# Attention and two FFN layers on one core: one local-attention tile moves from TensorE blocks to VectorE, and the hand-written order list is laid out anew

## The chip, the cores and the metric

The kernel runs on one core of one Trainium2 chip. The metric is the device time of one execution in microseconds (us). PE is TensorE, DVE VectorE, ACT ScalarE, POOL GpSimd, and SP is SyncE, which issues most of the DMAs. Lower is better.

## The reference

The attention works on q, k and v of shape (4 batches, 8 heads, 576 positions, 64 channels). Its output is the sum of two parts, and two FFN layers follow:

```python
q_d, k_d, v_d = (z.reshape(B, H, 144, 4, D).mean(axis=3) for z in (q, k, v))
out_up = np.repeat(sm_attn(q_d, k_d, v_d), 4, axis=2)        # pooled attention
mask = np.abs(pos[:, None] - pos[None, :]) < 4               # local attention, 7 keys a query
out_local = softmax(np.where(mask, 0.125 * q @ k.T, -1e9)) @ v
x = (out_up + out_local)                                     # as (2304 tokens, 512)
x = np.maximum(x @ w_in, 0) ** 2 @ w_out                     # 2048 hidden channels
y = ((x @ w_a) * (x @ w_b)) @ w_out2                         # 1536 hidden channels
```

## The kernel before, in words

The 2304 tokens are nine attention tiles of 256 (i = 0 to 8). The first FFN takes them in pairs, `TILES = ((0, 2), (2, 2), (4, 2), (6, 2), (8, 1))`: four FFN tiles of 512 tokens and a last one of 256. For FFN tile t and each of 16 slices f of the hidden channels, `hidden` (token `H.t.f`, twelve matmuls of 128x512, L650) makes the hidden values, `highs` and `lows` (`J`, `L`) split them into two parts on ACT and DVE (L657 to L665), and `project` (`P.t.f`, twelve matmuls, L685) adds them into four PSUM banks, which `evict` (`E`) and `store` (`D`) move out. Then comes the second layer (L932 and around it), which the change touches only in which of its preparing steps (`F`, after `V.n` in numbered slots) stand where.

Local attention has two forms. `Block` works on PE: it loads queries, keys and values of two channel pairs cp (`bq`, `bv`), makes scores (`bs`, 16 matmuls a call, L530), a masked softmax on DVE, ACT and POOL (`bm`, `bx`, `be`, `bd`, `bn`; `be` is eight exponentials, L559), transposes (`bt`, 4 a call, L581, copied by `bc`), multiplies by the values (`bw`, 32 a call, L593), adds the pooled part (`bo`, `ba`) and splits into high and low (`bh`, `bl`). One tile has 4 calls of `bs`, 4 of `bt` and 2 of `bw`. `Local` works on DVE: for each of four heads it multiplies queries by a window of keys (`lm`, L418, 128x1792), reduces (`ls`, L426), and after a softmax (`lx`, `le`, `lz`) multiplies by a window of values (`lv`, L458); POOL adds the seven products up in three steps (`lw`, L468 to L470); PE transposes the result (`lt`, 4 matmuls, L476, two calls a tile), DVE adds the pooled part (`la`, L485), and it is split (`lh`, `ll`, L492, L498). It loads through `lk`, `lu` and `lb`. Tiles 0 to 4 are blocks and 5 to 8 local before the change (`BLOCKS = 5`).

Pooled attention runs per batch b: the four members of each group are added up in DRAM order by four DMAs, the first on SP (L264), the other three on POOL as accumulating DMAs that wait for one another (`pa.b.n.j`, L262; n = 0 is queries and keys together, n = 1 values). Batch 0 loads them apart and adds on DVE and POOL (`pg`, `pj`). Then `pq` scales, and `ps` (8 matmuls, L287), `px`, `pe`, `pd`, `pn`, `pt` (4, L338), `pc`, `pw` (8, L352), `po` follow. FFN tile t needs attention tiles 2t and 2t + 1, and the batches that lie in them.

The weights of the first FFN come as 64-bit words and are decoded by `wd` (the load, L215, into rings of a few buffers), `wc`, `wa` (L224), `wh`, `wl` (L235). `Z.k.n.kind` is n transposes of the identity (L872), which give nothing to the result.

What sets the order is the list `ORDER`. The program walks it from left to right and emits what each token names, with the letter at its end (A, V, G, S) choosing ACT, DVE, POOL or SP. Each engine runs its own instructions in that order and stops at one whose inputs or buffer aren't ready; SP does the same with its DMAs. `CTS` lets a pair of blocks take its channel tiles as 0, 1, 2, 3 and a pair of locals as 0, 2, 1, 3; FFN tile 2 (attention tiles 4 and 5) goes from the one to the other with the change.

Of the kernel before, what the change touches and what calls it, by code (L numbers as in the profile page):

```python
# [46 lines left out]
bs.1.0.0.5 wc.8.A wa.0 wh.0.G ps.0.0.1.6 wl.0.G ps.0.3.0.3 px.0.1.1 pe.0.1.1 bn.0.1.V px.0.2.1 ps.0.3.1.1 bv.0.0.S
px.0.0.0 pa.0.1.2 wd.1.S pe.0.2.1 wd.15.S bm.1.0.0 bx.1.0 pd.0.2 pd.0.1 wd.2.S pe.0.0.0 bt.0.0.1.2 px.0.3.1 bv.1.0.S
be.1.0 bc.0.0.1.A bs.1.0.1.7 px.0.0.1 bs.1.1.1.0 wc.1.V wa.1 pn.0.1.G bd.1.0 bt.0.1.1.4 pe.0.0.1 bn.1.0.G Z.0.4.5
pa.0.1.3 px.0.3.0 bm.1.0.1 pd.0.0 wc.15.V pn.0.0.V pn.0.2.A pe.0.3.1 Z.6.4.6 wh.1.V bm.1.1.1 bt.1.0.0.5 pt.0.2.0.6  # L50
bw.0.0.7 pe.0.3.0 wl.1.G bc.1.0.0.A wa.15 wh.15.G pt.0.0.1.5 pt.0.0.0.1 bt.1.1.0.3 pd.0.3 pt.0.1.0.2 bc.0.1.1.A bx.1.1
# [5 lines left out]
wh.17.G ba.1.1.V bh.1.2.A bh.0.2.A wa.5 bh.1.3.V bl.0.2.V bl.1.3.V bl.1.2.V H.0.0 wd.9.S bs.2.1.0.6 wh.5.V wl.5.V
H.0.1 J.0.0 bs.2.0.0.7 wc.3.V wa.3 wh.3.G wd.6.S bq.2.1.S wc.9.V wa.9 wl.3.V wd.10.S L.0.0 H.0.2 wa.4 wh.9.V P.0.0
wh.4.V wl.4.G wl.17.G J.0.1 wc.6.V L.0.1 H.0.3 wc.10.A wa.6 P.0.1 wl.9.G wh.6.A J.0.2 wd.7.S L.0.2 wl.6.G wc.7.A wa.10
wa.7 wh.7.V wl.7.G H.0.4 J.0.3 wd.11.S wh.10.G wl.10.V wc.11.V wa.11 wh.11.V wl.11.V pl.1 bm.2.1.0 wd.14.S L.0.3 P.0.2  # L60
wc.14.V H.0.5 wa.14 wd.13.S wd.12.S wc.12.A P.0.3 wh.14.G wl.14.V wc.13.A wa.13 J.0.4 wa.12 L.0.4 H.0.6 bm.2.0.0
wh.13.G wl.13.V wh.12.V wl.12.V bx.2.0 bs.2.1.1.7 wd.16.S wc.16.A wa.16 wh.16.G pa.1.1.0 pa.1.0.0 J.0.5 L.0.5 wd.19.S
H.0.7 P.0.4 P.0.5 wc.19.A be.2.0 wa.19 wd.24.S wd.22.S wh.19.V J.0.6 wc.24.V wa.24 L.0.6 pa.1.0.1 H.0.8 bd.2.0 P.0.6
bn.2.0.V bm.2.1.1 bs.2.0.1.6 J.0.8 wd.21.S wc.21.V pa.1.1.1 wa.21 L.0.8 bm.2.0.1 wh.21.A bx.2.1 wh.24.V wl.16.G
wl.19.G H.0.10 wd.18.S wd.20.S wd.25.S J.0.7 L.0.7 H.0.9 wl.21.G wc.20.A bt.2.1.0.7 pa.1.0.2 P.0.7 wc.18.A wa.18
wh.18.V wl.18.V P.0.8 wa.20 bc.2.1.0.A wc.22.V wh.20.G wc.25.A wl.20.G J.0.9 L.0.9 wa.22 H.0.11 wh.22.A P.0.9 wa.25
wh.25.V J.0.10 ps.1.0.0.7 wl.22.V wd.29.S L.0.10 wc.29.V wa.29 pa.1.0.3 pq.1.V ps.1.0.1.0 J.0.11 be.2.1 px.1.0.0
wl.25.G bt.2.0.0.6 bd.2.1 wd.26.S wl.24.V L.0.11 P.0.10 wd.23.S px.1.0.1 wc.26.A ps.1.1.0.1 wc.23.A P.0.11 wa.26
pe.1.0.1 bc.2.0.0.A pe.1.0.0 bn.2.1.G wa.23 wh.26.V bt.2.1.1.6 pa.1.1.2 wh.23.V wl.23.V bv.2.0.S bc.2.1.1.V bw.2.0.0
bo.2.0.A wd.27.S bq.3.0.S wc.27.A ps.1.1.1.7 bt.2.0.1.6 H.0.12 wa.27 bc.2.0.1.A px.1.1.0 bv.2.1.S wh.29.V bw.2.1.6  # L70
pe.1.1.0 pd.1.0 px.1.1.1 H.0.13 pn.1.0.A J.0.12 wd.28.S wh.27.V bo.2.1.V L.0.12 pe.1.1.1 wc.28.A wl.26.G ps.1.2.0.7
pt.1.0.0.6 pt.1.0.1.0 J.0.13 pc.1.0.0.A wl.27.V P.0.12 ps.1.2.1.6 pc.1.0.1.V wa.28 wd.31.S wh.28.A wc.31.V wa.31
pd.1.1 H.0.14 pn.1.1.V px.1.2.1 pe.1.2.1 pa.1.1.3 wl.29.G wl.28.V wd.30.S px.1.2.0 pe.1.2.0 wh.31.V wl.31.V L.0.13
pw.1.0.7 pt.1.1.1.1 wc.30.A pc.1.1.1.A po.1.0.A wa.30 pt.1.1.0.1 ps.1.3.0.7 ps.1.3.1.6 wh.30.A wl.30.G pd.1.2
pc.1.1.0.A pn.1.2.G P.0.13 px.1.3.1 px.1.3.0 J.0.14 bv.3.0.S bq.3.1.S pw.1.1.1 L.0.14 bs.3.1.0.0 pe.1.3.0 pe.1.3.1
po.1.1.A pd.1.3 ba.2.0.G bs.3.1.1.1 pt.1.2.1.7 pc.1.2.1.A bh.2.0.V bs.3.0.0.6 pt.1.2.0.7 bh.2.1.A pn.1.3.A pc.1.2.0.A
bm.3.1.1 bm.3.1.0 bm.3.0.0 bx.3.0 be.3.0 H.0.15 pt.1.3.1.6 bs.3.0.1.7 bm.3.0.1 pw.1.2.0 J.0.15 bx.3.1 bl.2.1.V
pc.1.3.1.A P.0.14 bd.3.0 pt.1.3.0.7 bn.3.0.V bt.3.0.0.6 be.3.1 bc.3.0.0.A pc.1.3.0.V L.0.15 bt.3.1.0.7 bc.3.1.0.V
pw.1.3.1 bw.3.0.6 P.0.15 po.1.3.V bd.3.1 pl.2 bl.2.0.V bn.3.1.V po.1.2.A pa.2.0.0 bq.4.0.S bv.3.1.S bt.3.1.1.0
pa.2.0.1 bo.3.0.A bt.3.0.1.1 pa.2.0.2 ba.2.1.V E.0.1.V pa.2.0.3 E.0.0.A pa.2.1.0 lu.20 bh.2.3.A bl.2.3.V ps.2.0.0.6  # L80
bc.3.0.1.A bc.3.1.1.V ba.3.0.V bs.4.1.0.7 bw.3.1.3 bh.2.2.A D.0.0 lk.22 Z.5.4.1 bl.2.2.V bh.3.0.V bs.4.0.0.2 bo.3.1.A
ba.3.1.V bh.3.1.A bh.3.2.A bm.4.1.0 ps.2.1.0.3 bl.3.0.G bh.3.3.A bl.3.1.G bl.3.3.V E.0.2.V bl.3.2.G pq.2.A bm.4.0.0
H.1.0 ps.2.1.1.7 H.1.1 J.1.0 px.2.1.0 pa.2.1.1 bx.4.0 L.1.0 H.1.2 pe.2.1.0 lm.5.2 J.1.1 be.4.0 px.2.1.1 E.0.3.V L.1.1
lk.20 bd.4.0 P.1.0 P.1.1 pe.2.1.1 H.1.3 ls.5.2 lm.5.0 J.1.2 L.1.2 bq.4.1.S ls.5.0 ps.2.0.1.7 D.0.1 H.1.4 bn.4.0.G
pa.2.1.2 P.1.2 px.2.0.1 lk.21 J.1.3 px.2.0.0 lm.5.1 L.1.3 ls.5.1 pa.2.1.3 H.1.5 pe.2.0.1 lk.23 J.1.4 L.1.4 pe.2.0.0
bt.4.0.0.7 H.1.6 P.1.3 pd.2.0 J.1.5 lm.5.3 P.1.4 ls.5.3 pd.2.1 bc.4.0.0.A lx.5 pn.2.0.G pt.2.0.0.6 bv.4.1.S bs.4.0.1.7
# [1233 lines left out]
```

## Time and profile before

| | us |
|---|---|
| median of 3 runs | 916.7 (916.36 to 917.46) |
| the profiled execution | 917.33 |
| its span, first to last instruction | 915.3 |
| PE busy | 884.0 |
| DVE, ACT, POOL busy | 567.0, 444.0, 305.5 |

The profiled execution lasted 2.0 us longer than its span. The first FFN begins at 53.3 us of the span (first matmul of L650), its FFN tiles 1, 2, 3 and 4 at 169.38, 278.72, 371.45 and 460.98, and the second layer at 512.95. The mean granted clock of PE, as a share of 2.4 GHz, is 0.81 over the first 53.3 us and 1.00 in every later stretch.

### The profile page before, as it was taken

The numbers are of one execution on the slowest core, as the hardware profiler recorded it, in microseconds if no ns is written. First come the engines' busy times: TensorE is split into PE (matmuls) and PEld (weight loads), VectorE is DVE, ScalarE is ACT, GpSimd is POOL, SyncE is SP. The second block draws the span as 40 slices with busy tenths as digits, with TensorE's granted clock in tenths as the row PEclk, the third lists the DMA queues.
The fourth block names the chain that finished last, engine by engine and source line by source line (L and its number), as shares of the span: only waits on it lengthen the run. The fifth ranks groups of instructions, "written<-read, shape, count | busy, mean of one in ns | idle before, by whom it ended". The sixth has DMA issues, their size and how long they took to land.

```text
span 915.3 us, 13995 instructions
## 1 busy us (share of the span) xinstructions
PE 884.0 (97%) x5032; PEld 734.3 (80%) x5032; DVE 567.0 (62%) x871; ACT 444.0 (49%) x1083; POOL 305.5 (33%) x293
## 2 busy tenths in 40 slices
...
GB/s 300 184 210 291 100 216 135 188 119 36 75 91 129 121 57 76 32 74 138 1 104 112 64 138 236 250 211 257 162 241 184 231 211 388 408 408 346 170 137 47
DMA packets 65181, 157.33 MB, mean 172 GB/s; under 512 B 7708, under 2 KB 10908, under 8 KB 65112
## 3 DMA queue, kind: packets, MB, share of 16 engines
...
q8 instruction: 39, 0.64, 0.3%
...
## 4 chain that ended last, share of the span: by engine, by line
PE 87%; DMA 4%; issue 3%; DVE 2%; ACT 2%; POOL 1%; SPq 0%; POOLq 0%; DVEq 0%; ACTq 0%
PE bank L932 42%; PE bank L650 20%; PE bank L685 20%; DMA vd<-in_v_p 1%; PE bank L593 1%; PE bank L287 1%; PE bank L352 1%; PE bank L530 1%; PE bank L581 1%; DMA vb<-in_v_t 1%; PE bank L338 1%; DMA qkd<-in_qk_p 1%; DMA kb<-in_k_t 1%; DMA yrs<-yr_d 0%; DVE p L418 0%
## 5 line engine op out<-in xcount | busy, mean ns | idle before, releaser
L932 PE MATMUL bank<-xb,wb 128*128 128x512 f32 x1008 | 230.1, 389 | 0.0
L932 PEld LDWEIGHTS bank<-xb,wb 128*128 128x128 f32 x1008 | 188.7, 188 | 39.2 <-ACT r L1011 0.3
L650 PE MATMUL bank<-xx,w 128*128 128x512 f32 (+1 forms) x960 | 214.4, 375 | 1.5 <-ACT xx L184 1.5
L685 PE MATMUL bank<-g,w 128*128 128x512 f32 (+1 forms) x960 | 210.3, 371 | 0.0
L650 PEld LDWEIGHTS bank<-xx,w 128*128 128x128 f32 x960 | 165.9, 189 | 35.8 <-ACT xx L184 2.6
L685 PEld LDWEIGHTS bank<-g,w 128*128 128x128 f32 x960 | 166.4, 189 | 31.3 <-issue 0.6
L932 PE MATMUL bank<-op,wo 128*128 128x512 f32 (+1 forms) x648 | 132.5, 366 | 2.5 <-DVE op L733 1.6
L932 PEld LDWEIGHTS bank<-op,wo 128*128 128x128 f32 x648 | 112.0, 189 | 23.1 <-DVE op L733 2.3
L665 DVE TENSOR_TENSOR g<-bank,g 128x512 fp32r<-128x512 f32 (+1 forms) x80 | 50.7, 634 | 111.2 <-PE bank L685 80.4
L733 POOL TENSOR_TENSOR wb<-raw,wb 128x256 fp32r<-128x256 f32 x96 | 77.9, 830 | 72.4 <-ACT wb L812 69.1
L657 ACT ACTIVATE bank<-bank 128x512 f32<-128x512 f32 (+1 forms) x80 | 43.5, 544 | 101.3 <-PE bank L650 100.2
L1011 ACT ACTIVATE r<-bank 128x512 f32<-128x512 f32 x72 | 43.0, 597 | 84.5 <-PE bank L932 75.6
L733 DVE TENSOR_TENSOR op<-ys,op 128x512 fp32r<-128x512 f32 x84 | 54.0, 706 | 31.3 <-ACT op L736 31.3
L660 ACT ACTIVATE g<-bank 128x512 fp32r<-128x512 f32 (+1 forms) x80 | 44.4, 555 | 58.4 <-PE bank L685 57.3
L224 DVE SCALAR_TENSOR_TENSOR raw<-raw,signs 128x512 uint32<-128x512 uint32 x68 | 54.9, 814 | 17.5 <-ACT signs L184 17.0
L965 DVE TENSOR_TENSOR r<-bank,r 128x512 f32<-128x512 f32 x48 | 32.9, 686 | 47.4 <-PE bank L932 33.2
L736 ACT ACTIVATE op<-ys 128x512 fp32r<-128x512 f32 x84 | 47.1, 624 | 25.1 <-PE bank L932 15.7
L733 POOL TENSOR_TENSOR wos<-raw,wos 128x256 fp32r<-128x256 f32 x48 | 43.9, 928 | 31.9 <-ACT wos L812 28.6
L468 POOL TENSOR_TENSOR pv<-pv 128x768 f32<-128x768 f32 x16 | 33.8, 2114 | 59.7 <-DVE pv L458 59.7
L658 ACT ACTIVATE bank<-bank 128x512 f32<-128x512 f32 (+1 forms) x80 | 43.1, 539 | 2.5
L184 ACT ACTIVATE signs<-raw 128x512 f16<-128x512 bf16 x54 | 40.6, 783 | 7.1 <-DVE raw L224 3.6
L804 DVE TENSOR_TENSOR raw<-raw 128x256 f32<-128x256 f32 x72 | 42.1, 609 | 0.8
(120 smaller groups left out, 984.0 us busy)
## 6 DMA issues: line engine op xcount, KB each, us to landing
...
```

Source lines behind the costliest of these rows:

```text
L224: nc.vector.scalar_tensor_tensor(out=self.v, in0=self.v, scalar=13, in1=self.signs, op0=ALU.logical_shift_right, op1=ALU.bitwise_or,)
L650: nc.tensor.matmul(out=h, lhsT=wi[f].w[:, a, ct * P:(ct + 1) * P], rhs=xT[t, ct][:, b], start=(n == 0), stop=(n == 3 * NCT - 1),)
L657: nc.scalar.activation(out=h, in_=h, func=AF.Relu)
L658: nc.scalar.activation(out=h, in_=h, func=AF.Square)
L660: nc.scalar.activation(out=self.g[0], in_=h, func=AF.Copy)
L665: nc.vector.tensor_tensor(out=self.g[1], in0=h, in1=self.g[0].bitcast(F32), op=ALU.subtract)
L685: nc.tensor.matmul(out=x2[t][et], lhsT=wo[f].w[:, a, et * P:(et + 1) * P], rhs=g[b], start=(f == 0 and (a, b) == (0, 0)), stop=(f == F1 - ...
L733: engine.tensor_tensor(out=out, in0=in0, in1=in1, op=ALU.subtract)
L736: nc.scalar.activation(out=tile_hi, in_=src, func=AF.Copy)
L804: nc.vector.tensor_tensor(out=self.of(key), in0=self.of(a), in1=self.of(b), op=op)
L932: nc.tensor.matmul(out=out, lhsT=blk[:, a, cols:cols + P], rhs=rhs[b], start=(start and n == 0), stop=(stop and n == 2), skip_group_check= ...
L1011: nc.scalar.activation(out=r[n][:, w], in_=bk["X", w], func=AF.Copy)
```

## The change

`BLOCKS` goes from 5 to 4, so attention tile 4 becomes a `Local`, and the whole list `ORDER` is new. Counted in the two lists: `bs` 20 and 16 calls, `bt` 20 and 16, `bw` 10 and 8, `lm`, `ls`, `lv`, `lw` 16 and 20 each, `lt` 8 and 10. `H`, `P`, the pooled tokens and the weights are as many as before. From `H.0.0` on, the small matmuls of attention stand between the large ones of the FFN in 46 runs before and 30 runs after. Of eight `Z` seven stood ahead of `H.0.0`, after the first scores, and one (`Z.5.4.1`) just ahead of `H.1.0`; after, four lie ahead of the first scores and the other four before `H.0.0`. Cut to what the text speaks of (the order of the first loads and of the first steps; the surroundings of `H.1.0`; the end of FFN tile 1):

```diff
-BLOCKS = 5
+BLOCKS = 4
...
-wd.17.S pc.0.0.0.A bc.1.1.0.A pc.0.0.1.V wa.8 bw.1.0.3 pw.0.0.5 pt.0.1.1.0 wl.15.V be.1.1 pc.0.1.1.A pc.0.1.0.V
-bv.0.1.S po.0.0.V wh.8.A wc.2.A pt.0.2.1.2 pw.0.1.5 pn.0.3.G bd.1.1 wa.2 bw.0.1.1 pc.0.2.1.A pc.0.2.0.A po.0.1.V
...
+Z.0.4.1 bq.0.0.S Z.5.4.3 pl.0 Z.1.4.7 Z.2.4.4 bq.0.1.S bs.0.0.0.0 bm.0.0.0 bs.0.1.0.6 bm.0.1.0 pa.0.1.0 bq.1.1.S
+pa.0.1.1 pg.0.0.0.S bq.1.0.S pg.0.1.1.S bs.0.0.1.7 bs.0.1.1.6 pg.0.0.3.S bx.0.0 Z.7.4.2 be.0.0 bs.1.1.0.1 pg.0.0.1.S
+sg pj.0.0.1.G bm.0.0.1 bm.0.1.1 bx.0.1 bv.0.0.S bd.0.0 bs.1.0.1.7 bn.0.0.V be.0.1 pg.0.1.3.S pg.0.1.2.S bt.0.1.0.2
+bs.1.0.0.0 ps.0.2.0.5 bd.0.1 bn.0.1.G pg.0.0.2.S bt.0.0.0.3 bt.0.0.1.4 bt.0.1.1.6 pj.0.0.2.V bc.0.1.0.V pg.0.1.0.S
+bm.1.0.1 bc.0.0.0.A pj.0.1.1.G bm.1.1.0 bm.1.0.0 pj.0.0.3.V pj.0.1.2.V pj.0.1.3.G pq.0.A bc.0.1.1.A bc.0.0.1.A
...
+px.0.3.0 pe.0.3.0 bn.1.0.G pt.0.0.0.2 pe.0.1.0 pc.0.0.0.A pt.0.0.1.3 bt.1.0.0.2 wl.0.V wd.8.S bx.1.1 pa.0.1.3 bv.1.1.S
+pn.0.2.G pt.0.2.0.1 wc.1.V wd.7.S wa.1 Z.6.4.7 pd.0.1 be.1.1 Z.4.4.4 pn.0.1.G pc.0.0.1.V px.0.3.1 bt.1.1.0.3 pw.0.0.5
+pt.0.1.0.7 wh.14.G pe.0.3.1 bc.1.0.0.V bd.1.1 pd.0.3 pt.0.2.1.4 bn.1.1.G bq.2.0.S bq.2.1.S pt.0.1.1.0 pn.0.3.V
...
+bw.1.0.0 pw.0.3.1 bh.0.1.A bv.0.1.S wa.8 bl.0.1.V bh.0.0.A bl.0.0.V po.0.2.A bw.0.1.7 wl.1.G wd.11.S ba.1.0.V bh.1.0.V
...
+bo.3.1.A bh.3.0.V bl.3.0.V ba.3.1.V bh.3.3.A bh.3.1.V bl.3.3.V bl.3.1.V ps.2.1.0.7 bh.3.2.A bl.3.2.V H.1.0 pa.2.0.2
+lm.4.0 E.0.2.A E.0.3.A H.1.1 pa.2.0.3 ls.4.0 J.1.0 pq.2.V ps.2.1.1.6 L.1.0 E.0.1.A px.2.1.0 H.1.2 pa.2.1.1 J.1.1 L.1.1
...
+H.1.15 P.1.13 J.1.14 L.1.14 P.1.14 pa.3.0.2 lt.5.1.0 lv.5.1 lw.5.0 lw.5.1 lt.5.0.6 D.0.1 lh.4.0.1 pa.3.0.3 J.1.15
+L.1.15 ll.4.0.1 lh.4.0.0 pa.3.1.0 lk.31 ll.4.0.0 la.5.1 lh.5.1.1 P.1.15 ll.5.1.1 la.5.0 lh.5.1.0 ll.5.1.0 pq.3.G lu.25
+lh.5.0.1 ll.5.0.1 lh.5.0.0 ll.5.0.0 H.2.0 lm.6.2 J.2.0 ps.3.0.0.7 H.2.1 E.1.0.A ps.3.0.1.6 L.2.0 H.2.2 J.2.1 L.2.1
...
+la.6.1 lh.6.1.1 ll.6.1.1 lh.7.0.0 lh.6.1.0 lh.7.0.1 ll.7.0.1 ll.7.0.0 la.7.1 E.2.3.A lh.7.1.0 E.2.0.V ll.7.1.0
```

Before the change the list around the same places reads:

```
bc.3.0.1.A bc.3.1.1.V ba.3.0.V bs.4.1.0.7 bw.3.1.3 bh.2.2.A D.0.0 lk.22 Z.5.4.1 bl.2.2.V bh.3.0.V bs.4.0.0.2 bo.3.1.A
...
H.1.0 ps.2.1.1.7 H.1.1 J.1.0 px.2.1.0 pa.2.1.1 bx.4.0 L.1.0 H.1.2 pe.2.1.0 lm.5.2 J.1.1 be.4.0 px.2.1.1 E.0.3.V L.1.1
```

## Rows read from the trace of the kernel before

**Rows 1.** Windows of the span: start, length, each engine's busy time (xinstructions), clock, DMA.
```profile
0.00:53.30 53.30, 34.65 (x413) 28.56 (x413) 33.61 (x73) 28.78 (x120) 19.85 (x23) 0.81 0.84 251
53.30:169.38 116.08, 114.20 (x809) 90.28 (x805) 76.99 (x147) 70.99 (x197) 34.86 (x33) 1.00 0.67 185
169.38:278.72 109.34, 106.50 (x620) 83.39 (x617) 71.99 (x92) 49.17 (x134) 35.71 (x30) 1.00 0.39 96
278.72:371.45 92.73, 91.43 (x457) 73.33 (x457) 73.13 (x87) 40.65 (x107) 46.02 (x29) 1.00 0.35 94
512.95:915.30 402.35, 395.75 (x1945) 335.28 (x1943) 248.49 (x384) 190.58 (x391) 136.25 (x150) 1.00 0.63 230
```

**Rows 2.** The chain that ended last, around 40 us: start, length, what.
```profile
37.67 0.33 SPq L215
...
38.04 7.03 DMA vb<-in_v_t
...
45.12 1.98 PE bank L593 x32
```

**Rows 3.** PE's timeline, 78 to 91 us: start, busy us, line, shapes, count, idle before.
```profile
78.67 2.96 PE L650 MATMUL bank<-xx,w 128*128 128x512 f32 x12
81.47 2.89 PE L685 MATMUL bank<-g,w 128*128 128x512 f32 x12
84.20 2.96 PE L650 MATMUL bank<-xx,w 128*128 128x512 f32 x12
87.09 0.70 PE L530 MATMUL bank<-kb,qb 64*64 64x70 f32 x16
87.73 3.06 PE L650 MATMUL bank<-xx,w 128*128 128x512 f32 x12
90.63 1.76 PE L685 MATMUL bank<-g,w 128*128 128x512 f32 x7
```

**Rows 4.** PE's timeline, 196 to 226 us: small matmuls alone and in a run.
```profile
196.81 0.60 PE L581 MATMUL bank<-ident,blk 128*70 128x128 f32 x4
197.16 3.03 PE L650 MATMUL bank<-xx,w 128*128 128x512 f32 x12
...
219.99 1.15 PE L593 MATMUL bank<-blk,vb 70*64 70x64 f32 x32
...
223.94 1.03 PE L581 MATMUL bank<-ident,blk 128*70 128x128 f32 x8
224.91 0.71 PE L352 MATMUL bank<-aT,vd 72*64 72x144 f32 x8
```

**Rows 5.** PE's timeline where tile 5's transposes stand.
```profile
263.37 0.66 PE L476 MATMUL bank<-ident,x 128*128 128x128 f32 x4 [0.99 <-POOL x L470]
...
276.46 0.66 PE L476 MATMUL bank<-ident,x 128*128 128x128 f32 x4 [1.47 <-POOL x L470]
```

**Rows 6.** POOL's timeline, 150 to 165 us: an accumulating DMA of pooled batch 2.
```profile
163.53 0.86 POOL L262 DMA_DIRECT2D qkd<-in_qk_p  x1 [5.16 <-DMA qkd<-in_qk_p]
```

**Rows 7.** POOL's timeline, 257 to 328 us: additions of `lw`, beside DVE and apart.
```profile
259.56 2.95 POOL L469 TENSOR_TENSOR pv<-pv 128x512 f32<-128x512 f32 x1
...
323.00 1.83 POOL L468 TENSOR_TENSOR pv<-pv 128x768 f32<-128x768 f32 x1 [10.80 <-DVE pv L458]
324.91 1.29 POOL L469 TENSOR_TENSOR pv<-pv 128x512 f32<-128x512 f32 x1
326.28 0.75 POOL L470 TENSOR_TENSOR x<-pv 128x256 f32<-128x256 f32 x1
```

**Rows 8.** DVE's timeline beside the first row of Rows 7.
```profile
259.33 2.04 DVE L458 TENSOR_TENSOR pv<-vt,sc 128x1792 f32<-128x1792 f32 x1
```

**Rows 9.** Groups by line, whole span: busy us, mean ns, idle before.
```profile
L418 DVE TENSOR_TENSOR p<-qt,kt 128x1792 f32<-128x1792 f32 x16 | 35.8, 2242 | 0.6 <-DMA kt<-in_k_l 0.5
L458 DVE TENSOR_TENSOR pv<-vt,sc 128x1792 f32<-128x1792 f32 x16 | 33.7, 2109 | 4.3 <-POOL x L470 4.2
L426 DVE TENSOR_REDUCE sc<-p 128x28 f32<-128x1792 f32 x16 | 32.0, 2007 | 0.2
```

More of the change, by code (lines that the diff above doesn't have):

```diff
@@ L47 @@
[L47 to L51, printed above, removed]
@@ L57 @@
[L57 to L61, printed above, removed]
@@ L62 @@
[L62 to L86, printed above, removed]
@@ new lines @@
+wh.11.G wh.7.V wd.2.S wl.11.V wc.2.A J.0.0 wl.7.V L.0.0 pa.1.0.0 bs.2.1.1.7 H.0.2 wd.9.S pa.1.0.1 wd.4.S wa.2 wh.2.A
+wl.2.G bm.2.1.0 wl.14.G wc.5.V wa.5 J.0.1 P.0.0 wh.5.A wc.4.A L.0.1 wa.4 wl.5.V wh.4.G H.0.3 wl.4.V J.0.2 L.0.2
+wd.16.S bx.2.0 H.0.4 wc.9.A P.0.1 wd.6.S wc.6.V wa.6 wh.6.A wl.6.G J.0.3 P.0.2 wd.10.S wd.12.S wa.9 L.0.3 wh.9.G
+wl.9.V H.0.5 wc.12.V pa.1.0.2 P.0.3 be.2.0 bm.2.0.1 J.0.4 wa.12 wh.12.G L.0.4 H.0.6 wc.10.A wa.10 wh.10.V wl.10.V
+P.0.4 wl.12.V pa.1.0.3 bd.2.0 wc.16.A pq.1.G J.0.5 L.0.5 P.0.5 bn.2.0.V wd.13.S wd.18.S wc.13.V wa.13 wh.13.V wl.13.V
@@ new lines @@
+wh.24.A wl.24.V wa.27 L.0.9 pn.1.0.G wc.21.V wa.21 P.0.9 pt.1.0.0.1 bt.2.0.1.6 J.0.10 L.0.10 bo.2.0.A ps.1.2.0.7
+pt.1.0.1.0 wh.21.A wl.21.V wd.23.S pc.1.0.0.A bc.2.0.1.A wc.23.V wa.23 wh.23.V wd.25.S wl.23.V bt.2.1.1.1 wh.27.A
+pc.1.0.1.V ps.1.2.1.6 H.0.12 bc.2.1.1.V H.0.11 wd.22.S px.1.2.1 px.1.2.0 pd.1.1 pn.1.1.V wc.22.A J.0.12 wl.27.V wa.22
+wh.22.V wl.22.V P.0.10 J.0.11 pa.1.1.2 wd.30.S wc.30.V wa.30 bq.3.0.S wc.25.A wh.30.V wl.30.V L.0.11 P.0.11 L.0.12
+wa.25 pe.1.2.1 bw.2.1.6 pe.1.2.0 wd.28.S pa.1.1.3 bs.3.1.0.1 pt.1.1.0.7 wh.25.V wc.28.V wa.28 bo.2.1.A wl.25.G
@@ new lines @@
+bm.3.1.0 bs.3.0.0.0 pd.1.2 pw.1.0.6 pt.1.1.1.1 pn.1.2.G pc.1.1.1.A wh.28.G bm.3.0.0 wd.26.S H.0.14 pc.1.1.0.V po.1.0.V
+wc.26.A bx.3.0 wa.26 wh.26.A wd.29.S pw.1.1.6 wl.26.V wc.29.V wa.29 pt.1.2.1.7 wh.29.G wd.31.S be.3.0 pc.1.2.1.V
+wl.29.V po.1.1.V H.0.13 ba.2.0.G wl.28.V ps.1.3.0.6 P.0.12 J.0.13 lk.17 bh.2.0.V L.0.13 ps.1.3.1.7 pt.1.2.0.1 J.0.14
+pc.1.2.0.A px.1.3.0 P.0.13 bq.3.1.S px.1.3.1 pe.1.3.0 pe.1.3.1 pw.1.2.1 L.0.14 wc.31.V wa.31 bs.3.0.1.6 pd.1.3
+pn.1.3.V po.1.2.A bs.3.1.1.1 pt.1.3.0.0 bd.3.0 bn.3.0.V bm.3.0.1 pt.1.3.1.7 pc.1.3.0.A bm.3.1.1 pc.1.3.1.A bt.3.0.0.6
```

100 lines of the change are left out of this document (53 added, 47 removed).

## The prediction

> **What bounds the kernel now.** I read the windows by stage first, then the chain of waits, then PE's timeline, and last the groups by line. The windows [rows 1] show that PE is the limit from the first FFN on: between 53.3 and 371.45 us it is busy for 312.13 of 318.15 us, so only 6.0 us there are idle, and in the second layer for 395.75 of 402.35. DVE is next, with 71.99 of 109.34 us in FFN tile 1 and 73.13 of 92.73 in tile 2. Only the first 53.3 us are different: PE is busy for 34.65, DVE for 33.61, ACT for 28.78, so no engine fills that stage and its end is a matter of waits. The chain shows which one [rows 2]: SP sits behind a weight load (L215, `wd.17`) until 37.67, issues the value load `bv.0.1` at 38.04, the values land 7.03 us later, and at 45.12 PE goes on with `bw.0.1` (L593). So two things can move the time: the matmuls that PE does between 53.3 and 513 us, and the waits of the first stage.
>
> **PE's matmuls.** I price a call by the distance from its start to the next start. `H` takes 2.80 us and `P` 2.73 among large ones. An `H` ahead of a small call takes 2.89 and one behind it 2.90 [rows 3], so a run of small calls costs 0.09 + 0.10 = 0.19 us beside its own work. A `bs` takes 0.64 [rows 3]. Four transposes alone take 0.35, two calls in a row 0.97, so the second costs 0.62 [rows 4]; `lt` has the same four 128-wide transposes. A `bw` takes 1.15 at most [rows 4].
> - Block 4 out: 4 x 0.64 = 2.6 for `bs`; three lone `bt` and one behind a small call, 3 x 0.35 + 0.62 = 1.7; 2 x 1.15 = 2.3 for `bw`. Together -6.6.
> - `lt.4` in: both calls follow each other, 0.35 + 0.62 = +1.0.
> - `Z.5.4.1` leaves the place ahead of `H.1.0` for the start: -0.6, a second call of four transposes.
> - `bs.2.0.0` and `bs.2.1.0` go ahead of `H.0.0`: -1.3 here. There PE has 18.65 idle us to take them in [rows 1]; without that cover they cost the 1.3 again.
> - 46 runs become 30: 16 x 0.19 = -3.0 at best. But in the new list 7 more calls of transposes (block 4 left aside) stand behind another small one, and each then costs 0.62 rather than 0.35: +1.9. If the first is real and the second not it is -3.0, the other way +1.9; I take the middle, -0.5.
>
> Sum -8.0 us, with bounds -10.5 and -5.6. PE is 97 to 99% busy in these stages [rows 1], so nothing hides this: it is on the path.
>
> **What DVE and POOL get in its place.** Local tile 4 costs DVE 4 x (2.24 + 2.01 + 2.11) = 25.4 us for `lm`, `ls` and `lv` [rows 9] and some 5 more for its softmax, sums and splits; block 4's DVE work, some 9 us, goes (both estimates, from the numbers of their short calls). Two heads' `lm` and `ls` of tile 6 (8.5 us) that ran in FFN tile 1 move into FFN tile 2, and two of tile 8 (8.5 us) move from tile 2 to tile 3. So DVE in FFN tile 1 rises from 72 to about 85 of some 105 us, and in tile 2 it stays near 73. POOL gains four heads of 1.83 + 1.29 + 0.75 = 3.9 us [rows 7], 16 us on 36 of 109. Neither is full, so PE's pace hides both as a sum. What isn't hidden is the last link: today tile 5's two `lt` already keep PE waiting for POOL, 0.99 and 1.47 us [rows 5]. In the new list both `lt` of tile 5 stand just ahead of `P.1.15` and `H.2.0`, and tile 7's last one right ahead of `H.3.0`, with one large call or none to cover `la`, `lh` and `ll`.
>
> A second tight place is new. Pooled batch 2 is summed by one load and three accumulating DMAs, each of which POOL holds for 0.86 + 5.16 = 6.0 us until the next can start [rows 6]. The first may go when `ps.1.3.1` has read the buffer; with some 5 us for it (an estimate from the 5.16 that POOL waited for one) the chain is 5 + 3 x 6.0 = 23 us. Between `ps.1.3.1` and `ps.2.1.1` the new list has three `P` (8.2), three `H` (8.4) and small calls of about 8.6 us, 25 in all. `pq.2` now stands on DVE, behind `ls.4.0`, and while it waits for that DMA the next `px`, `lm` and `L` wait too; before, ACT did it. Margin 2 us, so 0 to 4 us late.
>
> Bounds for PE's waits in this stretch: 6.0 us before; none of it comes back if the places are as tight as now, and all of it goes if the list is right. I take +1 for `ps.2` and +1.5 for the two FFN tile starts, in sum +2.5, with -4 and +10 as ends (ten is four waits like the longest seen, 1.47, and one missed accumulation of 6).
>
> **A rule against the change.** Beside `lv` on DVE (259.33, 2.04 us) the POOL addition L469 takes 2.95 us, and 1.29 us with no such neighbour [rows 7, 8]: it ends 1.14 us after `lv` does, about its own length. The Trainium skill (SBUF — State Buffer, Who interferes with whom) says that a DVE instruction with two SBUF inputs and a GpSimd one that reads SBUF never share: the later one waits for the whole of the first. The trace agrees in that place. By the rule the 16 new `lm` and `lv` calls would at worst each push a POOL addition or be pushed by one.
>
> **The first stage.** The new SP order has `wd.8` behind a buffer that `wl.3` frees, then `bv.1.1`, `wd.7` behind `wl.0`, `bq.2.0`, `bq.2.1`, and then `bv.1.0` and `bv.0.1`. The wait behind a weight buffer thus stays, but PE wants `bv.0.1` last of all the attention's loads, and the `wl` that frees the buffer comes earlier in DVE's order (0.3 + 7.03 us to gain at most [rows 2]). Against that, 1.1 MB of `bq.2` now lie ahead of those values; at the 251 GB/s of this stage [rows 1] that is 4.4 us. 7.4 - 4.4 = 3.0; I take -2.5. The other end is +3: the pooled keys' first part (`pg.0.1.0`) is now the last of the pooled loads, and three joins have to follow it before `ps` can start, in DVE's and POOL's turn. The four `Z` at the head run before the scores; the mean clock is 0.81 here [rows 1], and if the low stretches move it changes small matmuls only, which is within this range.
>
> **Moved past each other, at no cost.** On SP `lk` and `lu` of tile 4 stand ahead of the stores `D.0.0` and `D.0.1`; the next evictions (`E.1`) need the staging buffers only at `H.2.0`, some 15 us later by the calls between. The second layer gets the same instructions in nearly the same slots: 0 +- 1.5 us.
>
> **Sum.** -8.0 + 2.5 - 2.5 = -8.0 us on the profiled execution's 917.3 (span 915.3 and 2.0 around it) is 909.3. That execution lies 0.6 above the median of the runs, so the median should be 908.7, say 909.
>
> **Rivals.**
> 1. *The start gives all its wait back.* `bv.0.1` lands before PE wants it: -7.4 in place of -2.5, 904. For it: `bw.0.1` is the last attention call. Against: 33.61 us of DVE work in chains with ACT. Chance 0.15.
> 2. *The saved matmuls become waits, and the start gains nothing.* One accumulation of 6.0 us arrives late at `ps.2`, and -2.5 becomes 0: -8.0 + 2.5 + 5 = -0.5 to -2, 915. For it: the 2 us margin. Against: in FFN tile 2 before, PE waits 1.3 us in all [rows 1]. Chance 0.22.
> 3. *DVE and POOL shut each other out, slower.* With two local tiles in FFN tile 1, 8 heads x 3.9 = 31 us of POOL additions and about 34 us of `lm` and `lv` exclude each other. If all of POOL's time stopped DVE, 85 + 31 = 116 us would stand against 105, +11 at `H.2.0`; tile 2 shifts by the late start of tile 6's heads, some +3. Then -8.0 + 14 - 2.5 = +3.5, 920. It decides once PE waits more than 10.5 us longer at L476 and the `H` behind it than the 2.5 of before [rows 5]. For it: the stretched row [rows 7]. Against: FFN tile 2 carried the same eight heads with DVE at 73 of 93 us. The skill's rule named above is this mechanism. Chance 0.13.
> 4. *The new grouping of small calls isn't cheaper*: +1.9 in place of -0.5, 911. It is in the forecast's own range.
>
> **Chances.** Forecast 0.50 (its own range 904.5 to 913), rivals 0.15, 0.22 and 0.13. A run of this kernel can be told from no change beyond about 0.2%, 1.8 us. Faster by more: forecast and rival 1 whole, and half of rival 2, 0.76; within: 0.09; slower: rival 3 and a rest of rival 2, 0.15. The range 902 to 919 leaves out the far ends of rivals 1 and 3.
>
> **What would show it.** Right: first L650 near 51 us and the chain without a 7 us DMA on `vb`; 256 matmuls of L530, 64 of L581, 256 of L593 and 40 of L476; the stretch from the first L650 to the second layer some 5 us shorter than 459.7; PE idle there about 8 us. Step by step: `ps.2.1` behind `H.1.1` waiting for a DMA or for DVE's `pq` is the second tight place; L476 waiting for L470 just ahead of tiles 2 and 3 is the first; an `H` still at 2.90 behind a small call, and 30 such places, is the run's price. Wrong: PE idle above 16 us in that stretch, or a first L650 later than 56 us.

## The result and the profile after

After the change the kernel takes 903.74 us (median of 4 runs, 903.01 to 904.06), against 917.08 for the kernel before on the same chip: a ratio of 0.9852, 95% interval 0.9835 to 0.9869. The profiled execution took 904.06, its span 902.3, so 13.0 us of span went. The forecast was 909 with a range of 902 to 919. The lines of the kernel after are those of before less one (L649 for L650, and so on).

The windows by stage, cut at the first FFN matmul and at the starts of FFN tiles 1, 2 and 3, and last the second layer; they answer to [rows 1] (the clock of the first row, 1.00, isn't what PE ran at there; the last section says why):

```profile
0.00:55.03 55.03, 37.37 (x449) 31.16 (x449) 32.72 (x68) 27.70 (x121) 19.93 (x24) 1.00 0.81 244
55.03:165.97 110.94, 110.39 (x736) 88.01 (x737) 83.67 (x158) 65.95 (x185) 31.77 (x31) 0.98 0.67 187
165.97:266.00 100.03, 99.14 (x497) 78.90 (x495) 78.87 (x93) 43.96 (x109) 40.80 (x32) 1.00 0.47 115
266.00:363.96 97.96, 97.95 (x497) 79.08 (x497) 77.41 (x90) 42.79 (x108) 44.77 (x29) 1.00 0.33 89
500.62:902.30 401.68, 395.64 (x1945) 335.44 (x1943) 246.68 (x382) 188.86 (x387) 136.34 (x149) 1.00 0.64 234
```

PE's idle time in FFN tiles 0 to 2, length less busy, is 0.55 + 0.89 + 0.01 = 1.5 us; it was 6.0 [rows 1]. FFN tile 2 became 5.2 us longer with PE never idle, because it took over calls (497 PE matmuls where it had 457); tile 3 became 4.7 shorter. The first stage became 1.7 us longer. The whole stretch from the first `H` to the second layer went from 459.66 to 445.59, by 14.1.

The chain of waits in the first stage; where [rows 2] had a 7.03 us DMA of `vb` just ahead of the end, there is none now, and the early part hangs on the pooled loads (`more`) and their join (L274):

```profile
3.58 6.29 DMA qb<-in_q_t
9.88 8.49 DMA more<-in_qk_p
...
18.52 0.10 POOL qkd L274
18.61 1.26 issue
19.88 1.12 POOL blk L571
21.05 1.72 PE bank L580 x7
...
41.44 1.71 PE bank L871 x8
...
49.78 0.65 DVE raw L223
50.43 0.34 DVE xx L620
50.80 0.39 ACT xx L183
```

PE's timeline at the two places that the prediction called tight (start, busy us, line, shapes, count, in brackets the idle time and what ended it): first `ps.2.1` behind `H.1.1`, then both `lt` of tile 5 (L475) and the start of FFN tile 2, which answers to [rows 5]:

```profile
172.21 0.71 PE L286 MATMUL bank<-qkd 64*72 64x144 f32 x8 [0.50 <-PE bank L649]
...
256.35 5.66 PE L684 MATMUL bank<-g,w 128*128 128x512 f32 x24
261.84 1.04 PE L475 MATMUL bank<-ident,x 128*128 128x128 f32 x8
262.63 2.98 PE L684 MATMUL bank<-g,w 128*128 128x512 f32 x12
266.00 5.73 PE L649 MATMUL bank<-xx,w 128*128 128x512 f32 x24 [0.39 <-ACT xx L491]
```

0.50 and 0.39 us are all that is left of waits above 0.3 between PE's calls behind the first `H` (before there were 0.99, 1.47, 0.56 and a 1.30 for `vd`). Some idle time also stands inside the first call of an FFN tile, whose inputs arrive in parts: before 1.17 in `H.0.0` and 0.30 in `H.1.0`, after 0.55 in `H.0.0` and 0.46 in `H.3.0`. `H.3.0` before and after:

```profile
371.45 2.95 PE L650 MATMUL bank<-xx,w 128*128 128x512 f32 x12
```

```profile
363.96 1.18 PE L649 MATMUL bank<-xx,w 128*128 128x512 f32 x4
365.41 0.73 PE L649 MATMUL bank<-xx,w 128*128 128x512 f32 x2 [0.28 <-ACT xx L491]
366.33 4.45 PE L649 MATMUL bank<-xx,w 128*128 128x512 f32 x18 [0.19 <-ACT xx L491]
```

With 0.46 idle and matmuls spread out between the waits, `H.3.0` takes 3.87 us where it took 2.79.

POOL's last additions for tile 5, and one of DVE's multiplications beside them; they answer to [rows 7, 8]:

```profile
255.06 2.41 POOL L469 TENSOR_TENSOR x<-pv 128x256 f32<-128x256 f32 x1
257.43 1.84 POOL L467 TENSOR_TENSOR pv<-pv 128x768 f32<-128x768 f32 x1
259.35 1.29 POOL L468 TENSOR_TENSOR pv<-pv 128x512 f32<-128x512 f32 x1
260.71 0.75 POOL L469 TENSOR_TENSOR x<-pv 128x256 f32<-128x256 f32 x1
```

```profile
254.44 2.42 DVE L457 TENSOR_TENSOR pv<-vt,sc 128x1792 f32<-128x1792 f32 x1
```

POOL ends what `lt.5.0` needs at 261.46 and PE comes to it in the middle of the L475 pair, near 262.3: it is on time by 0.8 us. The same form L469 takes 2.41 us beside DVE's L457 and 0.75 apart.

To see where the calls' time went I priced each call of PE in both traces by one rule: its start to the next start, less PE's idle time between them (idle time inside a call stays in its price). From the first `H` to the last `P` that makes 453.6 us of calls and 4.4 of waits before, 443.1 and 0.9 after:

| us | before | after |
|---|---|---|
| H, P | 206.8, 200.7 | 206.2, 199.2 |
| bs, bt, bw | 7.6, 5.6, 6.9 | 3.3, 3.9, 4.2 |
| ps, pt, pw | 8.1, 6.5, 7.7 | 7.8, 6.7, 7.7 |
| lt, Z | 3.2, 0.6 | 4.2, 0 |

Block 4's own calls are 2.6 (`bs`), 1.8 (`bt`) and 2.2 (`bw`) of the column before. The three calls `H.0.0`, `H.1.0` and `H.3.0`, with the idle time inside them, make 10.9 before and 11.6 after (4.42, 3.66, 2.79 and 4.91, 2.77, 3.87); all other `H` went from 196.0 to 194.6.

By neighbours (medians of the calls for 512 tokens, before and after): an `H` between large calls 2.80 and 2.79, ahead of a small one 2.81 and 2.84, behind one 2.87 and 2.89. A `bt` alone costs 0.36; inside a run 0.56 and 0.53, at its end 0.39 in both.

### The profile page after: what moved, and what is told of

It is laid out like the page before. It is cut to its first block, busy times and chain, and to the rows that moved or that the text cites. A ratio compares the mean times of both kernels' runs of the same rounds, so it can differ in the third digit from the quotient of the medians.

```text
span 902.3 us, 13703 instructions
## 1 busy us (share of the span) xinstructions
PE 876.7 (97%) x4896; PEld 731.8 (81%) x4896; DVE 590.2 (65%) x886; ACT 435.1 (48%) x1049; POOL 311.2 (34%) x294
## 4 chain that ended last, share of the span: by engine, by line
PE 92%; DVE 3%; DMA 2%; ACT 2%; issue 1%; SPq 0%; POOLq 0%; POOL 0%; DVEq 0%; ACTq 0%
PE bank L931 42%; PE bank L649 22%; PE bank L684 22%; PE bank L351 1%; DMA more<-in_qk_p 1%; PE bank L337 1%; PE bank L286 1%; PE bank L580 1%; DMA qb<-in_q_t 1%; PE bank L592 0%; PE bank L475 0%; DMA yrs<-yr_d 0%; PE bank L529 0%; ACT a L310 0%; ACT blk L558 0%
## 5 line engine op out<-in xcount | busy, mean ns | idle before, releaser
L649 PE MATMUL bank<-xx,w 128*128 128x512 f32 (+1 forms) x960 | 213.5, 375 | 3.0 <-DVE xx L620 1.6
L649 PEld LDWEIGHTS bank<-xx,w 128*128 128x128 f32 x960 | 167.6, 190 | 38.5 <-issue 3.1
L467 POOL TENSOR_TENSOR pv<-pv 128x768 f32<-128x768 f32 x20 | 40.5, 2027 | 99.3 <-DVE pv L457 92.3
L223 DVE SCALAR_TENSOR_TENSOR raw<-raw,signs 128x512 uint32<-128x512 uint32 x68 | 52.5, 776 | 17.3 <-ACT signs L183 16.7
L457 DVE TENSOR_TENSOR pv<-vt,sc 128x1792 f32<-128x1792 f32 x20 | 42.5, 2134 | 0.4 <-DMA vt<-in_v_l 0.2
L417 DVE TENSOR_TENSOR p<-qt,kt 128x1792 f32<-128x1792 f32 x20 | 41.8, 2092 | 1.4 <-POOL x L469 1.4
```

What stands on the lines that cost most here:

```text
L223: nc.vector.scalar_tensor_tensor(out=self.v, in0=self.v, scalar=13, in1=self.signs, op0=ALU.logical_shift_right, op1=ALU.bitwise_or,)
L457: nc.vector.tensor_tensor(out=p, in0=window(heads.pop(("v", 4 * self.i + h))), in1=self.s[:, :, h].unsqueeze(3).to_broadcast([P, FACTOR, W ...
L649: nc.tensor.matmul(out=h, lhsT=wi[f].w[:, a, ct * P:(ct + 1) * P], rhs=xT[t, ct][:, b], start=(n == 0), stop=(n == 3 * NCT - 1),)
```

## The experiments

Three theories of the price of calls were put to the test in the first three: A, that a run of small calls has a price of its own; B, the prediction's middle, that joining a run costs as much as it saves; C, that changing between small and large costs nothing.

**Fourteen calls more, alone.**

```diff
-P.0.0 ... H.0.3
+P.0.0 ... Z.9.4.1 H.0.3     (and at 13 more places)
```

> The changed kernel with 14 more calls of four transposes of the identity, each alone between two large calls, just ahead of an H of the FFN tiles 0 to 2 that had a large call before it (30 runs of small calls become 44). A call alone takes 0.35 us by its own start to the next, and the large calls around it 0.19 more. Theory A (a run of small calls has a price of its own): 14 x (0.35 + 0.19) = +7.6 us. Theory B, the prediction's middle, in which a second small call in a row costs 0.62: the same +7.6 here, it differs in the next kernel. Theory C (going between small and large calls costs nothing): 14 x 0.35 = +4.9.

**The same fourteen in runs.**

```diff
-bs.2.1.1.7 H.0.2
+bs.2.1.1.7 Z.9.4.0 H.0.2     (and at 13 more places)
```

> The same 14 calls, each just ahead of an H of the same tiles that already stands behind a small call, so that the runs stay 30. Theory A: a call that joins a run costs only its own 0.28 to 0.53 us (the spread of such calls in the changed kernel's trace), some 0.4: +5.6, that is 2.0 less than the 14 alone. Theory B: 0.62 each, +8.7, or 1.1 more than alone. Theory C: +4.9 in both.

Alone: 914.85 us (912.66 to 916.43), ratio to the kernel before 0.9949 (0.9930 to 0.9967). In runs: 913.32 (912.54 to 913.67), 0.9931 (0.9911 to 0.9950). PE's timeline at one such place of each:

```profile
66.23 2.89 PE L685 MATMUL bank<-g,w 128*128 128x512 f32 x12
68.95 0.60 PE L872 MATMUL bank<-ident 128*128 128x128 f32 x4
69.70 4.66 PE L650 MATMUL bank<-xx,w 128*128 128x512 f32 x19
```

```profile
61.07 1.01 PE L530 MATMUL bank<-kb,qb 64*64 64x70 f32 x32
62.01 0.66 PE L872 MATMUL bank<-ident 128*128 128x128 f32 x4
62.73 3.06 PE L650 MATMUL bank<-xx,w 128*128 128x512 f32 x12
```

By the call prices the calls grow by 10.5 us alone (0.645 for each `Z`, and 0.11 for each `H` that now stands behind a small call) and by 9.7 in runs (0.69 for each `Z`, nothing for the large calls). All three theories had the `Z` itself too cheap, at 0.35; why it costs more than a lone `bt` was not tried. What tells them apart is the difference: 0.8 us in favour of runs, where A said 2.0, C 0 and B 1.1 the other way (the medians differ by 1.5, less than their spread). B falls. The 0.8 itself lies between A and C; what speaks against C is where it arises: the `H` calls cost 1.5 us more with the `Z` alone and nothing more with them in runs. So going between small and large has a price, for this kind of call smaller than A's 0.19.

**The runs split up again.**

```diff
-bs.2.1.1.7 H.0.2
+H.0.2 bs.2.1.1.7     (and 15 more such places; runs 30 -> 46)
```

> The changed kernel's list with 16 places at which one small call and one large neighbour trade places (11 single calls of bs, bt, ps, pt, pw and lt go behind the next H or P, two take their copy along, three P go behind the first small call that follows): the work is the same, the runs of small calls become 46 again, as before the change. Theory A: 16 x 0.19, less some 0.05 for each call that now stands alone: +2.2 us. Theory B: 16 x (0.19 + 0.35 - 0.62) = -1.3. Theory C: 0. A wait that opens because a result comes 2.8 us later would add to each.

914.52 us (913.38 to 916.50), 0.9949 (0.9931 to 0.9967), by the ratios some 9 us slower than the changed kernel. In its trace calls cost 5.3 us more (`H` 3.1, `P` 2.2, the small ones about nothing) and waits between calls 6.0 more. One of them, with the windows of the wait and of the 4.4 us behind it:

```profile
227.64 0.71 PE L351 MATMUL bank<-aT,vd 72*64 72x144 f32 x8
230.09 4.61 PE L649 MATMUL bank<-xx,w 128*128 128x512 f32 x12 [1.73 <-DVE g L664]
```

```profile
228.35:230.09 1.74, 0.01 (x2) 0.01 (x1) 1.63 (x4) 0.93 (x5) 0.00 (x0) 1.00 0.00 0
230.09:234.50 4.41, 4.41 (x12) 3.41 (x13) 3.72 (x4) 0.62 (x4) 1.39 (x1) 0.61 0.11 17
231.00:234.00 3.00, 3.00 (x9) 2.32 (x8) 3.00 (x3) 0.00 (x0) 0.89 (x1) 0.50 0.00 0
234.50:238.00 3.50, 3.50 (x22) 2.85 (x21) 3.36 (x6) 2.06 (x4) 2.60 (x3) 1.00 0.20 72
```

That `H` is 1.7 us longer than in the changed kernel, at a granted clock of 0.61 in the mean: the last two rows show 0.50 for most of its time and 1.00 after it. Without it 3.6 us remain for 16 runs, 0.23 each, near A's 0.19 for attention's own small calls. The waits, larger than the price, I had allowed for and not sized.

**POOL does more.**

```diff
+            if self.i == 4:
+                nc.gpsimd.tensor_copy(out=p[:, :, 4:7], in_=p[:, :, 0:3])
```

> In each of the four heads of local tile 4, after the first addition on POOL, POOL also copies 128x768 numbers onto the part of the products that is no longer read: 4 x 1.83 us more for POOL in FFN tile 1, beside DVE's lm and lv. If DVE and POOL do not bind there (what the changed kernel's trace suggests: DVE 78.87 and POOL 43.96 of 100.03 us): 0 to +0.5 us. If they shut each other out on the path (the prediction's rival 3): the copies push DVE or the last additions ahead of tile 5's transposes, +4 to +7 at the first H of FFN tile 2.

908.11 us (905.82 to 908.89), 0.9870 (0.9847 to 0.9894). A copy took 0.83 us, not 1.83, so POOL had 3.3 us more; still FFN tile 1 took 104.5 us in place of 100.0 (one trace of each; by the ratios the whole kernel is 1.7 us slower, with intervals that overlap). PE around tile 4's transposes (L477 here), and the windows of the wait and behind it:

```profile
239.95 1.10 PE L477 MATMUL bank<-ident,x 128*128 128x128 f32 x8 [2.11 <-POOL x L471]
```

```profile
237.90:239.90 2.00, 0.00 (x0) 0.00 (x0) 1.42 (x1) 0.00 (x0) 2.00 (x2) 1.00 0.03 13
241.60:246.00 4.40, 4.40 (x14) 3.52 (x13) 3.75 (x5) 2.35 (x5) 4.24 (x3) 0.62 0.83 138
```

The wait is 2.11 us and the `P` behind it 1.55 longer, again at a mean of 0.62. Neither side is right as put: DVE is no fuller than before (77.9 us), so it isn't a matter of their sums; but POOL's last link has next to no margin (in the changed kernel its addition for `lt.4.1` ends at 237.84 and PE comes at 238.05), and two of the final additions are stretched from 0.75 to 2.4 us beside DVE, the one that PE waits for among them.

**The start of before.**

```diff
-Z.0.4.1 bq.0.0.S Z.5.4.3 pl.0 ... bs.2.0.0.6 bs.2.1.0.3 ... H.0.0 ... H.0.1 ... bs.2.0.1.6
+bq.0.0.S bs.0.0.0.0 bs.0.1.0.6 Z.4.4.5 ... H.0.0 bs.2.0.0.6 ... H.0.1 bs.2.1.0.3 ... bs.2.0.1.6
```

> Everything ahead of the first H in the order that it had before the change (its loads, joins, scores and seven Z; the weights that it decodes there renamed to those that the changed list wants next), behind that the changed list; the two scores calls of block 2 stand behind the first two H again. Theory A (the changed start is the later one by itself, 55.03 us against 53.30 for its first H): the first H near 53.3, -1.7 us, of which the two scores calls take some 1.3 back, in all -0.4 to -1.0. Rival B (the start is late only because it decodes other weights and loads more of block 2 for what follows): the first H at 53.3, but the time comes back as waits in FFN tile 0, 0 to +2.

903.44 us (903.01 to 903.85), 0.9840 (0.9827 to 0.9853). The first `H` comes at 53.67, `P.0.0` at 66.13 with the same work done ahead of it; the changed kernel had `P.0.0` at 66.65 and, in the profile below, 65.88. The two starts can't be told apart: what the two `bs.2` calls save behind the first `H`, the changed start takes back ahead of it.

**The form alone.** In this kernel the addition for channel tile 3 of tile 4 stands ahead of batch 2's last pooled output, so that part is missing from its sum.

```diff
 (the list of before to H.2.0, without bs.4 to bl.4)
+lm.4.0 ls.4.0 ... lt.4.1.6 lt.4.0.7 ... lt.5.1.0 lt.5.0.6     (at the changed list's counts of H and P)
```

> Tile 4 local in a list that is otherwise the one of before up to the first H of FFN tile 2 (start, order of H and P, blocks 0 to 3, pooled batches 0 to 2), with the changed list's local work at the same counts of H and P and the changed list from H of tile 2 on; 38 runs of small calls. PE's calls by the prediction's prices: -6.6 + 1.0 = -5.6 for the block, and 8 runs less, 8 x 0.19 = -1.5 by theory A or nothing by theory B; the start as before. Against 917.1: 910 (A) or 911.5 (B) if the waits stay as before the change; 4 us less if the change of the form takes the waits at tile 5's transposes away, and up to 6 us more if the mixed list is late somewhere that neither list was.

937.09 us (931.57 to 939.63), 1.0198 (1.0173 to 1.0223): 19 us slower than the kernel before beside it. PE at tile 5's second `lt` and at FFN tile 2:

```profile
281.40 0.66 PE L475 MATMUL bank<-ident,x 128*128 128x128 f32 x4 [3.83 <-POOL x L469]
...
290.92 1.65 PE L649 MATMUL bank<-xx,w 128*128 128x512 f32 x3 [4.52 <-ACT xx L491]
```

FFN tile 1 takes 122.38 us there, PE busy for 106.26. So block 4's matmuls are saved, and the saving and more is lost, far beyond the "up to 6" that I allowed. In the trace, which is of the fastest of the six executions and 14.5 us longer than the one before, waits between PE's calls behind POOL, ACT and DVE make 15.5 us instead of 4.4, and the `H` calls, above all the first of each FFN tile, take 8.1 more. The mixed list isn't one that anybody laid out, so the 19 says nothing of what the form costs in a good one; it shows that the gain needs the list.

**Two tries at the changed start.**

```diff
-pj.0.0.1.G ... bn.0.1.G ... pj.0.0.2.V bc.0.1.0.V ... bm.1.0.1 ... pq.0.A ... be.1.0
+bn.0.1.G pj.0.0.1.G ... bc.0.1.0.V bm.1.0.1 bm.1.1.0 bm.1.0.0 bx.1.0 ... pj.0.0.2.V ... be.1.0 pq.0.A
```

> The changed kernel with two kinds of steps moved in the first stage: on POOL the first join of the pooled keys goes behind the multiplication of block 0's second half, on DVE the masks, the minimum of block 1 and a copy go ahead of the first join, and on ACT the exponentials of block 1 go ahead of the scaling of the pooled queries. Theory A (the start is late because an engine that stands at a join waits for a load, 6.80 us on POOL and 7.57 on DVE, with ready work of block 0 and 1 behind it): the first H 2 to 4 us earlier, 900 to 902. Rival B (the pooled chain itself, from the last landing at 18.4 us on, sets the end): 0, or a little later, as its first join then stands behind other work.

```diff
-bq.0.1.S ... bq.1.1.S ... pg.0.0.0.S bq.1.0.S pg.0.1.1.S ... bv.0.0.S ... pg.0.1.0.S
+bq.0.1.S ... pg.0.0.0.S pg.0.1.1.S ... pg.0.1.0.S bq.1.1.S bq.1.0.S bv.0.0.S
```

> The changed kernel with SP's loads of block 1 (queries and keys of both pairs) and of block 0's first values moved behind all pooled loads, and block 1's first three scores calls and masks behind the first pooled scores. Theory A (the pooled loads' place on SP makes the start late: the first pooled scores at 27.42 us, at 21.65 before the change): the first pooled scores near 22 to 24 us and the first H 2 to 4 us earlier, 900 to 902. Rival B (block 1's chain or the decoding of weights on DVE ends as late): 0. Rival C: block 1 now comes last, +1 to +3.

904.77 us (903.25 to 905.60), 0.9849 (0.9835 to 0.9862), and 904.65 (902.25 to 905.95), 0.9850 (0.9834 to 0.9866): no gain from either, rival B in both. In the second the pooled scores begin at 21.23 us instead of 27.42 and the first `H` still at 54.72. The pooled path is not what sets the stage's end. The chain's last 10 us are additions, splits (L620, L183) and weight decoding (L223) on DVE in turn with ACT; what would shorten these was not tried.

**The changed kernel again, without Z, and with an early transpose.** The runs from here on share one chip, so their medians can be compared.

> The changed kernel itself, for its spread and as the one to compare the next three with. If the start depends on more than the list, its second FFN matmul call (H.0.1), at 59.94 us in the first profile and at 58.19, 58.76 and 59.52 in the profiles of three variants with the same first stage, comes anywhere between 58 and 60 again; if the list alone sets it, at 59.9.

904.68 us (903.38 to 905.47), 0.9831 (0.9798 to 0.9863); H.0.1 at 59.16. With the variants that share this first stage H.0.1 lies between 58.19 and 59.94 and the first `H` between 53.31 and 55.03 (seven executions, mean 54.1): the list alone doesn't set it.

```diff
-Z.0.4.1 ... Z.5.4.3 ... Z.3.4.5     (all eight left out)
```

> The changed kernel without any of the eight Z (the transposes of the identity, four at the head and four in the first stage). Theory A (Z only stands in PE's way in the first stage; the last three took 1.7 us from 41.4 us on): the first FFN begins up to 1.7 us earlier. Rival B (Z keeps PE's clock up, and without it small matmuls take their long durations for longer): +1 to +3. Rival C (the first stage ends with DVE and ACT, PE has room): 0.

906.25 us (905.05 to 908.35), 0.9845 (0.9809 to 0.9880). The same window of this kernel, and of the changed one beside it:

```profile
45.00:60.00 15.00, 14.95 (x173) 13.06 (x171) 10.49 (x23) 4.64 (x14) 3.35 (x3) 0.50 0.65 204
```

```profile
45.00:60.00 15.00, 12.86 (x191) 10.65 (x190) 12.56 (x28) 6.66 (x19) 4.90 (x5) 0.89 0.64 197
```

Without `Z` the clock stays at its lower level (0.50, 1.2 GHz) through the end of the stage, PE is full with fewer matmuls, and the first `H` comes at 57.68 instead of 54.25. Rival B, in its lower half: 1.6 us by the medians, whose intervals overlap. The 3.4 at the first `H` is from the slowest of the six executions, 2.1 above their median.

```diff
-L.1.14 P.1.14 pa.3.0.2 lt.5.1.0 lv.5.1 lw.5.0 lw.5.1 lt.5.0.6
+L.1.14 lv.5.1 pa.3.0.2 lw.5.0 lw.5.1 lt.5.0.6 P.1.14 lt.5.1.0
```

> The changed kernel with the later of tile 5's two transposes (lt.5.0) one large call earlier, ahead of P.1.14 instead of ahead of P.1.15; the engines other than PE keep their orders. In the changed kernel's trace POOL ends the last addition that it needs at 261.46 us and PE comes to it at 262.3, so the margin is 0.8. Theory A (that place is as tight as the prediction said, and only its position in PE's order took the old waits of 0.99 and 1.47 away): PE comes to it at about 259.1 and waits some 2.4 us, one more run of small calls costs 0.2, the 0.39 at H.2.0 goes: +2.2. Rival B (POOL's last addition follows PE's order by way of other engines and comes earlier too): 0 to +0.5.

907.24 us (906.00 to 910.85), 0.9864 (0.9829 to 0.9899): 2.6 slower than the changed kernel beside it, 2.2 expected by A. PE there (L475 is `lt.5.0`, the row below it the `P` behind), and the window behind the wait:

```profile
260.11 0.66 PE L475 MATMUL bank<-ident,x 128*128 128x128 f32 x4 [2.02 <-POOL x L469]
260.52 4.58 PE L684 MATMUL bank<-g,w 128*128 128x512 f32 x12
```

```profile
260.50:265.00 4.50, 4.50 (x16) 3.52 (x15) 0.00 (x0) 0.00 (x0) 0.36 (x1) 0.62 0.77 129
```

Theory A: the place is as tight as the prediction said, and one large call more ahead of it is what takes the wait away. In this trace FFN tile 1 is 3.8 us longer than in the changed kernel beside it; the wait is 2.0 of them and the slow `P` behind it 1.7. That `P` wasn't forecast, and the 0.39 at `H.2.0` grew to 0.81 instead of going, so the near match of the sums is partly luck.

**A version of the three hints.**

```diff
 (the start of before, as above)
-bw.2.0.7 J.0.9 ... L.0.9 ... P.0.9 pt.1.0.0.1     pq.2.V
+J.0.9 ... L.0.9 ... P.0.9 bw.2.0.7 pt.1.0.0.1     pq.2.A
```

> Everything ahead of the first H as before the change (as in the run with the old start), pq.2 on ACT instead of DVE, and bw.2.0 one large call later so that it joins the next run of small calls (29 runs). Against the changed kernel: the start -0.5 to -1.0 as the run with the old start showed, 0.2 to 0.5 of the wait at ps.2.1, and 0.2 for the run: -1.0 to -1.7. If the old start's gain was noise of the start: -0.5.

906.50 us (905.66 to 908.48), 0.9856 (0.9822 to 0.9890): not faster, by the medians 1.8 us slower than the changed kernel beside it. The wait at `ps.2.1` shrank to 0.27, but `bw.2.0`, one large call later, pushed the transposes behind it, and the next `H` waited for DVE's copy:

```profile
124.30 3.99 PE L649 MATMUL bank<-xx,w 128*128 128x512 f32 x16 [1.80 <-DVE aT L185]
```

No run here beats the changed kernel by more than its spread.

## Why the prediction was right, step by step

| term | predicted | measured |
|---|---|---|
| block 4's calls out | -6.6 | -6.5 |
| `lt.4`, `Z.5`, two `bs.2` | +1.0 -0.6 -1.3 | the same |
| 46 runs to 30 | -0.5 | -3.8 |
| PE's waits, with `H.0.0`, `H.1.0`, `H.3.0` | +2.5 | -2.8 |
| first stage | -2.5 | +1.7 (mean of seven executions +0.8) |
| second layer | 0 | -0.7 |
| sum | -8.0 | -13.0 |

The direction was right, and so was what carries it, that PE's calls are on the path: -11.2 where -8.0 stood and -10.5 was the far bound. Block 4 was priced almost exactly (2.6, 1.8 and 2.2 against 2.6, 1.7 and 2.3). Three other terms were wrong, and that the time fell inside the range is partly luck: the errors of the runs and the waits (8.6 us too slow) and of the start (4.2 too fast) offset each other in part. The time is that of rival 1, 904, but rival 1's mechanism didn't happen: the start gave nothing back.

**The runs.** The step that 7 more transposes behind a small call would cost 0.62 each failed. 0.62 was read from one pair in [rows 4]; over both traces a `bt` costs 0.36 alone, 0.53 to 0.56 inside a run and 0.39 at its end, so joining costs 0.03 to 0.2 and not 0.27, and a `pt` shows next to nothing of it (medians 0.22 to 0.36 alone, 0.25 to 0.28 behind a small call after the change). I took the middle of -3.0 and +1.9, and the truth lay beyond the -3.0: `H` -1.3, `P` -1.5, the `bs` and `bw` of blocks 2 and 3 -0.9, `ps`, `pt` and `pw` -0.1. That is 0.24 for each run, where 0.19 stood; not all of it need come from the runs, but split up again, the 16 runs cost 3.6 in calls, 0.23 each.

**The waits.** This step was wrong in sign, because I added new waits at the tight places and let none of the old ones go. The new ones came about as forecast: `ps.2.1` was late by 0.50 and 0.99 in two profiles (+1 expected), and the two FFN tile starts cost 0.39 ahead of `H.2.0` and 1.08 in `H.3.0` (+1.5 expected). But all of the old 0.99, 1.47, 0.56 and 1.30 went, and 0.9 in `H.1.0`. (The far end of +10 doesn't add up either: four waits of 1.47 and a missed accumulation of 6 are 11.9.) Tile 5's transposes are the tight place that I misjudged: they stand late enough in PE's order for POOL, by 0.8 us, and those of tile 4 by 0.2. That the mechanism is there, the early transpose and POOL's copies show: one call earlier, or 3.3 us of POOL more, and the wait is 2.0 or 2.1. I weighed the margin by what seemed late before, and not by POOL's end against PE's arrival.

**DVE and POOL.** Rival 3 didn't come true as a sum; DVE had 78.87 of 100.03 us, less than the 85 reckoned. Its single case is in the rows: L469 at 2.41 beside L457, 0.75 apart. By the Trainium skill (SBUF — State Buffer, Who interferes with whom) the later of the two waits for the whole of the other, and the trace agrees: the addition began 0.62 us into the multiplication and ended 0.61 behind its end. It holds for all 31 pairs of a `lw` addition and an `lm` or `lv` multiplication that overlap in the traces of before and after (in one the two begin within 0.01 us): whichever began later ended about its own length behind the end of the other (the three additions 1.70, 1.15 and 0.60 us, the multiplication 1.88). In these runs it told on PE only where POOL was the last link.

**The first stage.** This step failed. The wait for `vb` went, as said, but the first `H` came at 55.03 and not near 51; what took the wait's place is what the prediction had named as the other end, the pooled loads (POOL waits until 18.52 at the first join), but the second try at the start brought the pooled scores 6.2 us forward and the first `H` not at all. The chain that a profile shows is probably one of several that end nearly together here: taking 7 us out of it bought nothing. What does set the end stays open. The term is best put at 0 to 2.

So the time came out at 904 rather than 909 because the waits went 5.3 us better than their term, the runs 3.3 and the second layer 0.7, and the start 4.2 worse and block 4 0.1.
